# Order of the first loads, folds and weight conversions in a Fourier-mixing and ELU kernel

## The chip, the cores and the metric

The kernel runs on one core of a Trainium2 chip. The core has five engines that work side by side, each through its own list of instructions, in order: TensorE (PE in the profile; PEld is its weight load), VectorE (DVE), ScalarE (ACT), GpSimd (POOL) and SyncE (SP), which here issues most transfers. Transfers run on the core's 16 DMA engines. The metric is the device time of one execution, in microseconds. A kernel's time is the median of several runs.

## The reference

```python
# x: 8 x 3008 x 256 float32; w_in: 256 x 2048, w_out: 2048 x 256
X = np.fft.fft(x, axis=1)
X = np.fft.fft(X, axis=2)
t = X.real.astype(np.float32).reshape(8 * 3008, 256)
h = t @ w_in
g = np.where(h > 0.0, h, np.exp(np.minimum(h, 0.0)) - 1.0)
out = (g @ w_out).astype(np.float32)
```

The real part of a two-dimensional Fourier transform of each batch feeds a two-layer network with an ELU between the layers. The two weights come as 64-bit floating-point numbers, x as 32-bit ones.

## The kernel before, in words

**The transform.** The 3008 rows of a batch are folded. The row s, its mirror image and the two rows half a sequence away are added and subtracted, in both the sequence and the channel direction, so that four short products with cosine and sine matrices are enough. `load_x(b)` brings a batch as four tiles: xl0 and xl3 hold the forward rows and come through SyncE's queue (L197, L198, in `ahead`); xl1 and xl2 hold the backward rows and come by an indirect gather that GpSimd issues (L181, in `back`). `fold_x` makes, for each of the four, an even fold `e0` to `e3` and an odd fold `o0` to `o3` of 128 x 768 elements (all at L504), a copy of one column (`c0` to `c3`), and then the sums E0, E2, EO0, EO1 and O0, O2, EO2, EO3. For batch 0 all folds run on VectorE, in the order in which they are called; for the others they run on GpSimd, in between. `fold_first` adds up one extra channel (`xa`, `xg`, `xd`, `xe`), and a `Dft` multiplies a folded tile with a matrix `MC` (PSUM banks pA to pD, M or H): `x_even` from `xe`, `R_even` from EO0, `I_even` from EO2, `R_odd` from EO1, `I_odd` from EO3. `copy`, `unfold`, `plus` and `minus` bring the result from PSUM into the rings Rr, Ir and Rb.

**The weights.** The transform over the channels is worked into `w_in` instead: `fold_chunk(c)` multiplies the converted chunk c of `w_in` with a constant matrix CC on TensorE, and `put_chunk(c)` copies the result into Wc and Ws. A chunk of 256 columns is loaded raw (512 KB, L238) and converted from 64 to 32 bits in four steps:

- `fields` (VectorE, L256 and L262) cuts out exponent and mantissa.
- `power` (ScalarE) turns the exponent into a power of two; in all chunks but the first two more passes convert the integers.
- `round` joins the two halves of the mantissa: on VectorE in `w_in`'s chunk 0 (L287), on GpSimd in all others.
- `scale` sets the sign in the power (VectorE, L310) and multiplies, on VectorE in chunk 0 (L319), on GpSimd (L419) in the others. In the chunks of `w_in` from 1 on, GpSimd then makes a sum and a difference (`pair`), which `fold_chunk` reads.

**The network.** Work goes in slots. A slot takes 128 x 512 values: `mm_P` (H from Rr and Wc) and `mm_Q` (added to it, from Ir and Ws) on TensorE, `even_part` (E, VectorE, L811), `h_minus` (L821), four passes of ScalarE for the ELU, `g_plus` and `g_minus` (L837), then the products with `w_out` into pA to pD.

**What sets the order.** A hand-written schedule: `at(t, fn)` records each piece with a due time, and at the end all pieces are called in the order of the due times. Almost every instruction is pinned, so the due times settle only the order on each engine; waits are then set for the data. Before the schedule come 46 products of zeros on TensorE and the first loads:

```python
    w1_chunks[0].load()
    nc.sync.dma_start(out=CC, in_=CC_dr.ap())
    L_first, loads = load_x(0)
    for load in loads:
        load()
    load_mats(0, 0, (BE,))
    w1_chunks[1].load()
```

`load_rest` first has ScalarE copy a row of x and write one element of MC10, which holds back that load and the ones behind it until x has come.

Of the kernel before, what the change touches and what calls it, by code (L numbers as in the profile page):

```python
# [72 lines left out]
def _chan_consts():  # L73

    c = np.arange(128)[:, None]

    def block(fn, d):  # L80
        return fn(2.0 * np.pi * ((c * d[None, :]) % 256) / 256)

    even, odd = np.arange(0, 129, 2), np.arange(1, 128, 2)
    return np.concatenate(
        [
            block(np.cos, np.roll(even[:64], -1)),
            -block(np.sin, even[1:64]),
            block(np.cos, even[64:]),
            -block(np.sin, odd),
            block(np.cos, odd),  # L90
            block(np.sin, odd),
            -block(np.cos, odd),
        ],
        axis=1,
    ).astype(np.float32)
# [11 lines left out]
def kernel(  # L107
# [7 lines left out]
    nc = tc.nc  # L115
# [6 lines left out]
    CC_dr = nc.inline_tensor(_chan_consts(), name="chan_mats")  # L122
# [47 lines left out]
    def load_x(b):  # L170

        L = [
            spool.tile([128, 6 * ND], FP, tag=f"xl{j}", bufs=1, name=f"xl{j}")
            for j in range(4)
        ]

        def back(j, few):
            cols = slice(0, 2 * ND) if few else slice(2 * ND, 6 * ND)
            c = 1 if few else 2 if j == 1 and b == NB - 1 else 0
            pin(  # L180
                nc.gpsimd.indirect_dma_start(  # L181
                    out=L[j][:, cols],
                    out_offset=None,
                    in_=xflat,
                    in_offset=bass.IndirectOffsetOnAxis(
                        ap=ix[:, c : c + 1].bitcast(U32), axis=0
                    ),
                    element_offset=(b * SEQ + (HALF if j == 1 else 0)) * ND,
                )
            )  # L190
            if b == NB - 1 and j == 1 and not few:
                nc.gpsimd.dma_start(
                    out=L[1][0:1, 2 * ND : 5 * ND], in_=xrows(b, SEQ - 3, 1, 1, 3)
                )

        def ahead(j, row):
            nc.sync.dma_start(out=L[j][:, 0 : 4 * ND], in_=xrows(b, row, 4, 128, 4))  # L197
            nc.sync.dma_start(  # L198
                out=L[j][:, 4 * ND :], in_=xrows(b, row + 512, 2, 128, 2)
            )  # L200

        loads = [lambda n=n: back(2 - n // 2, n % 2) for n in range(4)]
        return L, loads + [lambda: ahead(3, HALF), lambda: ahead(0, 0)]


    CC = cpool.tile([128, 384], FP, tag="CC")
# [10 lines left out]
    class Chunk:  # L217
# [7 lines left out]
        def load(self):  # L225
            dst = self.dst()
            home = self.home
            if isinstance(home, tuple) and (wide or self.pairs):
                tag, bufs, size = home
                home = spool.tile([128, size], FP, tag=tag, bufs=bufs, name="raw")  # L230
            self.ab = home[:, 0:512]
            if not wide:
                nc.sync.dma_start(out=dst, in_=self.src)
                return
            words = home[:, 0:1024].bitcast(I32)
            self.raw = words.rearrange("p (n w) -> p n w", w=2)
            n = dst.shape[1]
            nc.sync.dma_start(  # L238
                out=words.rearrange("p (a b) -> p a b", a=n), in_=self.src.bitcast(I32)
            )  # L240
# [84 lines left out]
    def w1_dst(c):  # L325
        q, half = divmod(c, 2)
        if q not in w1:
            t = spool.tile([128, 1024], FP, tag="ot", bufs=2, name="w1")
            w1[q] = t.rearrange("p (h n) -> p h n", h=2)
        return w1[q][:, :, half * 256 : (half + 1) * 256]  # L330
# [17 lines left out]
    w1_chunks = [  # L348
        Chunk(
            moe_w_in[:, c * 256 : (c + 1) * 256].rearrange("(h p) n -> p h n", p=128),  # L350
            lambda c=c: w1_dst(c),
            IN_HOMES[c],
            IN_TMP[c],
            c > 0,
            c > 0,
        )
# [21 lines left out]
    def load_mats(ri, kodd, cuts=()):  # L378
        n = (2 * ri + kodd) * BW
        ends = (0, *cuts, BW)  # L380
        for a, z in zip(ends, ends[1:]):
            nc.sync.dma_start(
                out=MC[ri, kodd][:, a:z], in_=MC_dr.ap()[:, n + a : n + z]
            )
# [36 lines left out]
    def act(o, i, func=AF.Copy, **kw):  # L421
        pin(nc.scalar.activation(out=o, in_=i, func=func, **kw))  # L422
# [408 lines left out]
    def exp_neg(ap):  # L831
        act(ap, ap, func=AF.Exp, scale=-1.0)
# [270 lines left out]
    for _ in range(46):  # L1103
        mm(idle, zero, zero[:, 0:1].to_broadcast([128, 512]), True)
    exp_neg(warm)
    w1_chunks[0].load()
    nc.sync.dma_start(out=CC, in_=CC_dr.ap())
    L_first, loads = load_x(0)
    for load in loads:
        load()  # L1110
    load_mats(0, 0, (BE,))
    w1_chunks[1].load()
    nc.sync.dma_start(out=pick, in_=PK_dr.ap())
# [4 lines left out]
    def fold_now(keys):  # L1118
        for key in keys.split():
            ops[key, 0]()  # L1120

    def dft_now(d, par, tag):
        d.mms(par, bank(tag))
# [6 lines left out]
    def at(t, fn):  # L1130
        events.append((t, len(events), fn))
# [10 lines left out]
        for chunk in (w1_chunks[3], w2_chunks[1], w1_chunks[4], w2_chunks[2]):  # L1142
            chunk.load()

    at(-26.0, w1_chunks[0].fields)
    at(-25.9, w1_chunks[0].power)
    at(-25.8, w1_chunks[0].round)
    def begin_x_even():
        state["x_even"] = Dft(0, 0, 0, fold_first(L_first), ring=Rb, first=True)

    at(-25.6, w1_chunks[0].scale)
    at(-25.5, load_rest)
    at(-25.0, lambda: fold_now("e3 c3 e0 c0 e2 c2 E2"))
    at(-24.5, begin_x_even)
    at(-24.4, lambda: fold_now("e1 c1 E0 EO0"))
    at(-20.7, lambda: load_mats(1, 1))
# [6 lines left out]
    at(-13.08, lambda: dft_now(state["x_even"], 1, "pD"))  # L1163
    at(-13.0, lambda: dft_now(R_even, 0, "pA"))
    at(-12.9, lambda: dft_now(R_even, 1, "pB"))
    at(-11.1, lambda: fold_now("o3 o2 O2"))
    at(-11.0, lambda: state["x_even"].unfold())
    at(-10.96, lambda: fold_now("o0 o1 O0 EO2"))
    at(-10.95, R_even.copy)
    at(-10.94, R_even.unfold)  # L1170
    at(-10.9, R_even.plus)
# [7 lines left out]
    at(0.05, lambda: dft_now(I_even, 1, "M"))  # L1179
    at(0.6, lambda: state["x_even"].minus())  # L1180
    at(0.61, lambda: act(Ir[96:128, NE:RUN], Rb[96:128, NE:RUN]))
    at(0.72, w1_chunks[1].scale)
    at(1.3, lambda: fold_now("EO1"))

    T = PERIOD
# [279 lines left out]
```

## Time and profile before

| | |
|---|---|
| time | 1958.78 us, median of 3 runs (1958.31 to 1960.0) |
| span of the profiled execution | 1955.7 us |
| TensorE busy | 1937.6 us, 99% |
| VectorE busy | 1300.7 us, 67% |
| GpSimd busy | 1377.4 us, 70% |
| first product with real data | 13.80 us |
| mean granted TensorE clock | 0.997 of full speed |

The first rows are the whole; the change is in the first 40 us. Until about 37 us the DMA engines move some 400 GB/s without a pause: x, the matrices, and the first half of the weights. The first slots start at 29.7 us, and from about 60 us the profile repeats itself from slot to slot. In a line of the timeline the columns are start in us, duration in us, engine, line, operation, what is written and read, and the number of instructions; in brackets the idle time of the engine just before, and what ended it. When several instructions are in one line, the duration runs from the first start to the last end.

### The profile page before, as it was taken

The numbers are of one execution on the slowest core, as the hardware profiler recorded it, in microseconds if no ns is written. First come the engines' busy times: TensorE is split into PE (matmuls) and PEld (weight loads), VectorE is DVE, ScalarE is ACT, GpSimd is POOL, SyncE is SP. The second block draws the span as 40 slices with busy tenths as digits, with TensorE's granted clock in tenths as the row PEclk, the third lists the DMA queues.
The fourth block names the chain that finished last, engine by engine and source line by source line (L and its number), as shares of the span: only waits on it lengthen the run. The fifth ranks groups of instructions, "written<-read, shape, count | busy, mean of one in ns | idle before, by whom it ended". The sixth has DMA issues, their size and how long they took to land.

```text
span 1955.7 us, 26996 instructions
## 1 busy us (share of the span) xinstructions
PE 1937.6 (99%) x8912; PEld 1655.1 (85%) x8912; DVE 1300.7 (67%) x2396; ACT 864.8 (44%) x1671; POOL 1377.4 (70%) x1816
## 2 busy tenths in 40 slices
PE   7999999999999999999999999999999999999999
PEld 4788788888888888888888888888888888888887
DVE  6976666666666666676666666666666766667666
ACT  3654444444444444444444444444444444344443
POOL 2788668776687766777667876678667777456655
PEclk8999999999999999999999999999999999999999
DMA  8236120111211021010210102002020010100101
GB/s 309 66 25 55 18 65 18 33 28 23 48 20 44 13 41 33 18 44 14 54 23 14 46 13 59 12 19 55 9 54 11 20 22 15 17 12 11 23 10 24
DMA packets 263290, 70.25 MB, mean 36 GB/s; under 512 B 248606, under 2 KB 249522, under 8 KB 263152
## 3 DMA queue, kind: packets, MB, share of 16 engines
q1 hardware_dynamic: 257360, 55.69, 14.7%
q0 software_dynamic: 3616, 12.59, 2.0%
q8 instruction: 70, 1.15, 0.2%
q14 instruction: 68, 0.56, 0.1%
q10 hardware_dynamic: 2176, 0.26, 0.1%
HBM read 43.66 MB, written 24.80 MB: 35 GB/s over the span
## 4 chain that ended last, share of the span: by engine, by line
PE 95%; DVE 2%; POOL 1%; issue 1%; DMA 1%; ACT 0%; SPq 0%; DVEq 0%; POOLq 0%
PE H L410 38%; PE pB L410 16%; PE pC L410 16%; PE pD L410 16%; PE pA L410 8%; POOL WT L419 1%; DMA xl<-in_x_dram 1%; POOL w L419 0%; DVE E L811 0%; POOL G L419 0%; DVE G L837 0%; DVE pow L310 0%; DVE v L416 0%; DVE G L821 0%; ACT G L422 0%
## 5 line engine op out<-in xcount | busy, mean ns | idle before, releaser
L419 POOL TENSOR_TENSOR G<-G 128x256 f32<-128x256 f32 x1440 | 1034.8, 728 | 510.8 <-DVE G L837 341.2
L811 DVE SCALAR_TENSOR_TENSOR E<-Rb,wex,H 128x256 f32<-128x256 f32 x752 | 327.8, 477 | 540.8 <-PE H L410 535.8
L422 ACT ACTIVATE G<-H 128x512 f32<-128x512 f32 x376 | 224.5, 597 | 959.3 <-DVE G L821 959.3
L410 PE MATMUL H<-Ir,Ws 128*128 128x256 f32 x1504 | 388.0, 380 | 2.3 <-DVE E L811 2.3
L410 PE MATMUL H<-Rr,Wc 128*128 128x256 f32 x1504 | 387.1, 380 | 0.0
L410 PE MATMUL pC<-G,WT 128*128 128x256 f32 x1440 | 369.5, 379 | 0.0
L410 PEld LDWEIGHTS H<-Rr,Wc 128*128 128x128 f32 x1504 | 285.1, 190 | 55.7 <-issue 3.3
L410 PEld LDWEIGHTS H<-Ir,Ws 128*128 128x128 f32 x1504 | 278.7, 190 | 51.4 <-DVE E L811 5.5
L410 PEld LDWEIGHTS pC<-G,WT 128*128 128x128 f32 x1440 | 273.6, 190 | 37.2
L821 DVE SCALAR_TENSOR_TENSOR G<-E,H 128x512 f32<-128x512 f32 x376 | 256.8, 683 | 45.6 <-POOL G L419 7.1
L837 DVE SCALAR_TENSOR_TENSOR G<-G,H 128x512 f32<-128x512 f32 x376 | 255.8, 680 | 42.5 <-ACT G L422 42.5
L837 DVE SCALAR_TENSOR_TENSOR G<-M,G 128x512 f32<-128x512 f32 x376 | 256.6, 683 | 0.0
L422 ACT ACTIVATE G<-G 128x512 f32<-128x512 f32 x376 | 233.2, 620 | 0.0
L410 PE MATMUL pD<-G,w 128*128 128x256 f32 x784 | 229.4, 379 | 0.4 <-POOL G L419 0.4
L410 PE MATMUL pA<-G,w 128*128 128x256 f32 x784 | 229.3, 379 | 0.0
L410 PE MATMUL pB<-G,w 128*128 128x256 f32 x784 | 229.3, 379 | 0.0
L422 ACT ACTIVATE M<-G 128x512 f32<-128x512 f32 x376 | 224.3, 596 | 0.0
L422 ACT ACTIVATE M<-M 128x512 f32<-128x512 f32 x376 | 221.0, 588 | 0.1
L410 PE MATMUL pB<-G,WT 128*128 128x256 f32 x720 | 214.8, 380 | 0.3
L410 PE MATMUL pD<-G,WT 128*128 128x256 f32 x720 | 214.1, 379 | 0.0
L410 PEld LDWEIGHTS pD<-G,w 128*128 128x128 f32 x784 | 148.9, 190 | 21.0 <-POOL G L419 0.8
L410 PEld LDWEIGHTS pA<-G,w 128*128 128x128 f32 x784 | 149.0, 190 | 20.2
(148 smaller groups left out, 1420.7 us busy)
## 6 DMA issues: line engine op xcount, KB each, us to landing
out_dram<-ot SPq DMA_DIRECT2D x496, 32.0 KB
xl<-in_x_dram SPq DMA_DIRECT2D x16, 512.0 KB
xl<-in_x_dram SPq DMA_DIRECT2D x16, 256.0 KB
out_dram<-ot SPq DMA_DIRECT2D x256, 2.0 KB
Rb<-r SPq DMA_DIRECT2D x10, 376.0 KB
raw<-in_moe_w_in_dram SPq DMA_DIRECT2D x7, 512.0 KB
MC<-dft_mats SPq DMA_DIRECT2D x3, 943.5 KB
raw<-in_moe_w_out_dram SPq DMA_DIRECT2D x4, 512.0 KB
```

Source lines behind the costliest of these rows:

```text
L410: nc.tensor.matmul(out_, lhsT=lhsT, rhs=rhs, start=start, stop=stop, skip_group_check=True)
L419: pin(nc.gpsimd.tensor_tensor(out=o, in0=a, in1=b, op=op))
L422: pin(nc.scalar.activation(out=o, in_=i, func=func, **kw))
L811: nc.vector.scalar_tensor_tensor(out=S.E[:, c], in0=Rb[:, cols(i)], scalar=wex[:, f : f + 1], in1=S.H[:, c], op0=ALU.mult, op1=ALU.add,)
L821: nc.vector.scalar_tensor_tensor(out=two(S.G[:, 0:512])[:, :, ::-1], in0=two(S.E), scalar=2.0, in1=two(S.H), op0=ALU.mult, op1=ALU.subtract,)
L837: nc.vector.scalar_tensor_tensor(out=o, in0=e, scalar=-1.0, in1=h, op0=ALU.add, op1=ALU.max)
```

## The change

Three things move. On SyncE's queue, xl3 and xl0 of batch 0 come first, ahead of chunk 0 of `w_in` and of CC. On VectorE, the folds of these two tiles, even and odd (e3, o3, e0, o0), come ahead of the conversion of chunk 0, which is then laced with e2 and E2; on ScalarE the column copies c3 and c0 come ahead of chunk 0's power, and the row copy of `load_rest` comes behind c2. And for chunk 1 of `w_in` the `scale` step is due at -10.84 instead of 0.72: its sign (L310) comes in front of the first slot's `even_part` on VectorE instead of behind the second's. No instruction is added or taken away. The order on TensorE and on GpSimd is the same; on SyncE one weight load of the fifth chunk of `w_out`, which waits for a buffer, is now in front of batch 1's xl3 instead of behind it.

The purpose: VectorE is to fold x while it would be waiting for more of it, and GpSimd is to get the sign of chunk 1 in time.

```diff
-    w1_chunks[0].load()
-    nc.sync.dma_start(out=CC, in_=CC_dr.ap())
     L_first, loads = load_x(0)
     for load in loads:
         load()
+    w1_chunks[0].load()
+    nc.sync.dma_start(out=CC, in_=CC_dr.ap())
     load_mats(0, 0, (BE,))
...
-    at(-26.0, w1_chunks[0].fields)
-    at(-25.9, w1_chunks[0].power)
-    at(-25.8, w1_chunks[0].round)
+    at(-26.9, lambda: fold_now("e3 c3 o3 e0 c0 o0"))
+    at(-26.8, w1_chunks[0].fields)
+    at(-26.7, w1_chunks[0].power)
+    at(-26.6, lambda: fold_now("e2 c2"))
+    at(-26.5, w1_chunks[0].round)
+    at(-26.4, lambda: fold_now("E2"))
+    at(-26.3, w1_chunks[0].scale)
...
-    at(-25.6, w1_chunks[0].scale)
     at(-25.5, load_rest)
-    at(-25.0, lambda: fold_now("e3 c3 e0 c0 e2 c2 E2"))
     at(-24.5, begin_x_even)
     at(-24.4, lambda: fold_now("e1 c1 E0 EO0"))
...
-    at(-11.1, lambda: fold_now("o3 o2 O2"))
+    at(-11.1, lambda: fold_now("o2 O2"))
     at(-11.0, lambda: state["x_even"].unfold())
-    at(-10.96, lambda: fold_now("o0 o1 O0 EO2"))
+    at(-10.96, lambda: fold_now("o1 O0 EO2"))
...
-    at(0.72, w1_chunks[1].scale)
+    at(-10.84, w1_chunks[1].scale)
```

## The prediction, made before the changed kernel ran

> **What bounds the kernel now.** I read the page first (how busy the engines are), then the table by stages, then the timeline and the chain of waits of the first 60 us. The page says that TensorE is the bound of the whole:
>
> ```profile
> PE 1937.6 (99%) x8912; PEld 1655.1 (85%) x8912; DVE 1300.7 (67%) x2396; ACT 864.8 (44%) x1671; POOL 1377.4 (70%) x1816
> ```
>
> So only 18 us of the span are TensorE idle, and an edit that leaves the number of matmuls alone can win only there. The table by stages shows where they are (PE is the first busy time after the length of the stretch, PEclk the granted clock, then the DMA share and GB/s):
>
> ```profile
> 20.00:30.00 10.00, 6.88 (x25) 5.12 (x24) 9.60 (x18) 1.66 (x4) 0.00 (x0) 0.84 1.04 405
> 30.00:40.00 10.00, 4.77 (x18) 3.08 (x17) 7.85 (x14) 3.68 (x8) 4.59 (x4) 0.84 0.75 284
> 40.00:50.00 10.00, 9.73 (x40) 6.98 (x40) 6.63 (x13) 6.76 (x15) 4.54 (x5) 0.80 0.39 131
> 50.00:60.00 10.00, 9.71 (x47) 7.37 (x46) 10.00 (x17) 6.23 (x13) 6.31 (x6) 1.00 0.21 53
> 60.00:70.00 10.00, 9.98 (x50) 7.97 (x49) 9.06 (x16) 6.34 (x14) 9.30 (x9) 1.00 0.44 138
> ```
>
> From 20 to 40 us PE misses 8.4 us, from 60 on nothing. Besides, the clock is below 1.00 from 20 to 50. TensorE's own timeline shows the two gaps, and what they cost twice:
>
> ```profile
> 23.46 0.50 PE L410 MATMUL H<-pick,Ws 128*128 128x1 f32 x4
> 27.08 2.86 PE L410 MATMUL pC<-MC,o 128*128 128x189 f32 x6 [3.12 <-issue]
> ...
> 33.66 1.10 PE L410 MATMUL H<-Ir,Ws 128*128 128x256 f32 x4
> 40.27 1.12 PE L410 MATMUL H<-raw,CC 128*64 128x256 f32 x4 [5.50 <-POOL raw L419]
> ```
>
> After 3.12 us idle, six matmuls of I_even take 2.86 us; the same six of R_even take 1.28 in the chain of waits. After 5.50 us idle, the eight of fold_chunk(1) take 1.98 (later chunks: 1.08). The first gap ends when VectorE has made EO2 (26.98). The second is a chain in the timeline of all engines:
>
> ```profile
> 35.02 0.86 DVE L811 SCALAR_TENSOR_TENSOR E<-Rb,wex,H 128x256 f32<-128x256 f32 x2
> 35.80 0.68 DVE L310 SCALAR_TENSOR_TENSOR pow<-raw,pow 128x512 int32<-128x512 int32 x1
> ...
> 36.62 1.32 POOL L419 TENSOR_TENSOR w<-w,pow 128x512 f32<-128x512 f32 x1 [4.25 <-DVE pow L310]
> ```
>
> GpSimd sits idle 4.25 us for a sign that VectorE could have set once ScalarE's power was there (29.91). Then come product and pair (to 40.22), and TensorE. VectorE idles early instead, waiting for x:
>
> ```profile
> 9.05 0.96 DVE L504 TENSOR_TENSOR e<-xl 128x768 f32<-128x768 f32 x1 [1.30 <-DMA xl<-in_x_dram]
> 13.44 1.83 DVE L504 TENSOR_TENSOR e<-xl 128x768 f32<-128x768 f32 x2 [3.44 <-DMA xl<-in_x_dram]
> ```
>
> **What the Trainium skill says.** "TensorE: Matmul & The Clock Gate", Part 1: a free-running window of 3413 ns; after an idle window the array has half the clock, and a busy window gives it back. The trace agrees: read in stretches of 1 us, the clock falls at 26.86, returns at 30.27, falls at 37.10 and returns at 43.92, all multiples of 3.41 apart. It fell after windows with 0.5 and 1.1 us of work and not after one with 2.5; between lies the threshold. "SBUF — State Buffer", Who interferes with whom: a VectorE instruction with two SBUF inputs and a GpSimd instruction that reads SBUF block each other. The trace agrees: EO1 takes 1.48 us beside GpSimd, the same kind 0.96 alone. "DMA: Bandwidth & Descriptors", Queues, rings and completion order: an engine takes packets from its queues in turn, and each ring in order. That fits the landings below, which I use instead of a price.
>
> **Loads.** Landings of before, from what waited for them: the first weights (512 KB) at 4.8; with CC (192) and xl3 (768), 1472 KB in all, at 9.0; with xl0 (768), 2240 KB, at 13.4. GpSimd's gathers share the engines and are not moved. Straight lines between these points give the new order: xl3 (768 KB) 5.9, xl0 (1536) 9.4, first weights (2048) 12.3, CC 13.4. Estimates; plus or minus 1 us. Later loads keep place and bytes, except that xl3 of batch 1 goes behind a weight load that waits until after 35; its first use is after 80. Costs nothing.
>
> **VectorE.** By start-to-start times of before: e3 5.9, o3 6.9, e0 9.4, o0 10.35, done 11.3. These two odd folds (1.8 us) now lie in the old 4.7 us of idle. Then fields 12.35, e2 13.2, round 14.08, E2 14.75, sign 15.65, product 16.37, so w1 chunk 0 is ready at 17.06 (before: 7.75). fold_first to 17.5 (before 16.86), then e1, copy, E0, EO0 as before 3.14 us, to 20.64 (before 20.00). o2, O2 to 22.4, x_even's unfold to 22.9, o1, O0, EO2: R_even's unfold can start at 25.7 (before 26.90). VectorE by itself is 1.2 us ahead, though the even folds are 0.6 late. On ScalarE, copies for e3 and e0 lie in idle time; the row for x1 slips some 1.5 us, which MC10's load hides, as its user comes 12 us later.
>
> **A new wait.** fold_chunk(0) is the first real work on TensorE, and everything is queued behind it in order: x_even, R_even, I_even. The zero matmuls that keep it warm end at 13.87, so it now idles 3.2 us to 17.1. With the old window phase the window 13.21 to 16.62 has 0.66 us of work: half clock until 20.03. Sixteen matmuls need 0.248 us each then (from the eight at 40.27), 0.122 after: done 20.55. pC and pD 3.3 us as before, pA from 23.85, pB's end 27.05 (before 23.62). R_even.plus, which waits for pB, starts at 27.1 instead of 27.61: ahead by 0.5. At full clock it would be 1.2 (VectorE's bound); with weights 1 us late, 0.5 behind. I take 0.5 ahead. The old first gap closes: I_even follows at 27.4, warm.
>
> **The early sign.** 0.68 us on VectorE in front of E, which waited 1.33 us for wex (from ScalarE) anyway: free. The queue behind it is that E, then TensorE's first ring; none moves later. ScalarE's conversion ends at 30.5 (30.99 less 0.5), GpSimd adds 1.30, multiplies 1.30, pairs 2.20: fold_chunk(1) starts at 35.45, not 40.27. TensorE idles from 33.6 for 1.85 us instead of 5.50, so I take it as warm: fold 1.08, Q 1.03, R_odd's pA 1.3, turn 0.34, pB 2.0, to 41.2 (before 47.76); next P to 42.1. Its partners keep up: EO1 by 37.3, ScalarE's four ELU passes 38.1 to 40.2, G at 41.0, w2 chunk 0 on GpSimd at 40.5, all before TensorE asks at 42.1. VectorE: R_odd.unfold 41.0, plus and minus 41.6 to 42.6, sign of chunk 2, E at 43.3 to 44.2; the Q behind it starts at 44.3, before at 50.65. That is 6.35; I take off one GpSimd block of 0.52 (EO1's), so 5.8 us. From 60 on TensorE is full, and VectorE's work is in step with it: the shift stays to the end. 1958.8 - 5.8 = 1953.0.
>
> **Rivals.** (a) Half clock strikes again in the second gap (1.85 us is between the known cases; a half-clock window costs up to 1.7), or the first weights land late (1.0): together some 2.0 less, 1955.0. For: in the old phase that window has 1.65 us of work. Against: that's above the 1.1 which fell. (b) The wait only moves: VectorE, 100% busy from 50 to 60, becomes the bound. In 26 to 52 it is busy 20.2 of 26, so it can give at most 5.8, and if the waits on H and ScalarE stay, about a third: 1956.9. Against: those waits end with TensorE's and ScalarE's own work, which moves too. (c) Slower: the first weights' delay and a worse interlock of VectorE and GpSimd in the 50 us after, ten blocks of 0.5 and 5 more from the late fold_chunk(0): 10 lost against 5.8, 1963. Against: a delay of fold_chunk(0) is paid once, on a chain with over 3 us of old idle behind it. (d) No half clock at all: 1951.7.
>
> **Numbers.** Forecast 0.54, (a) 0.22, (b) 0.13, (c) 0.05, (d) 0.06. Faster by 0.2% means under 1954.9: forecast, (d) and half of (a), 0.71; same 0.24 (the rest of (a), (b)); slower 0.05. Range 1951.5 to 1957.0: it leaves out (c) and the edges. It covers weights late by 1 us, either clock state in both gaps, and up to two thirds lost to VectorE.
>
> **What would show it.** In the trace after: e3 and o3 before 8 us, the first weights' fields near 12.3, fold_chunk(0) near 17 with a clock below 1 behind it, I_even near 27.4 without a gap, fold_chunk(1) near 35.5, the Q of the third step near 44.5, and no idle of 0.5 us beyond that was not there before. Wrong, if fold_chunk(1) starts after 38, if TensorE waits for E or G by more than 1 us between 36 and 60, or if the lead at 60 us is not the lead at the end.

## The result and the profile after

| | before | after |
|---|---|---|
| time, median of 4 runs each | 1959.39 us | 1951.88 us |
| range of the runs | 1958.31 to 1960.21 | 1950.55 to 1953.88 |
| span of the profiled execution | 1955.7 us | 1952.1 us |
| start of the third step's Q in it | 50.65 us | 45.98 us |

The ratio is 0.9963, with an interval of 0.9946 to 0.998: 7.5 us less, and between 4 and 10.6 with the interval. A later comparison (e8 below) gave 6.3 us. The two profiled executions differ by less, 3.6 us: the one of before was quick (1957.48), the one of the changed kernel the slowest of its four (1953.88). The forecast was 1953.0, in a range of 1951.5 to 1957.0.

The page of the changed kernel: TensorE's work is the same to 0.4 us, the span is shorter.

```profile
span 1952.1 us, 26996 instructions
...
PE 1937.2 (99%) x8912; PEld 1654.7 (85%) x8912; DVE 1299.0 (67%) x2396; ACT 864.9 (44%) x1671; POOL 1379.2 (71%) x1816
```

The table by stages of the changed kernel (columns as before: length, busy time of PE, PEld, DVE, ACT and POOL, granted clock, DMA share, GB/s):

```profile
10.00:20.00 10.00, 6.55 (x31) 3.15 (x31) 8.18 (x17) 1.55 (x5) 0.00 (x0) 0.81 1.05 403
20.00:30.00 10.00, 10.00 (x39) 6.84 (x36) 7.82 (x14) 1.83 (x5) 0.00 (x0) 0.85 1.03 404
30.00:40.00 10.00, 8.75 (x42) 6.09 (x41) 8.74 (x20) 5.84 (x14) 5.30 (x6) 1.00 0.70 257
40.00:50.00 10.00, 8.72 (x39) 5.86 (x39) 9.90 (x18) 7.54 (x17) 5.91 (x6) 1.00 0.44 175
50.00:60.00 10.00, 10.00 (x47) 8.45 (x47) 9.06 (x16) 7.92 (x16) 7.25 (x6) 1.00 0.33 91
```

From 20 to 40 us TensorE misses 1.25 us instead of 8.35, but from 10 to 20 it now misses 3.45, where it had missed 1.24, and the half clock now begins there (a granted clock of 0.81, and of 0.85 from 20 to 30). From 40 to 50 VectorE is busy for 9.90 us of 10; whether it is the next bound is tried in e9. TensorE's timeline of the changed kernel:

```profile
17.08 3.68 PE L410 MATMUL H<-w,CC 128*64 128x256 f32 x16 [3.45 <-DVE w L319]
20.69 2.64 PE L410 MATMUL pC<-MC,xe 128*128 128x189 f32 x6
...
28.61 1.52 PE L410 MATMUL pC<-MC,o 128*128 128x189 f32 x6
...
34.13 1.10 PE L410 MATMUL H<-Ir,Ws 128*128 128x256 f32 x4 [0.36 <-DVE Ir L416]
36.12 1.08 PE L410 MATMUL H<-raw,CC 128*64 128x256 f32 x8 [0.89 <-POOL raw L419]
...
43.46 1.97 PE L410 MATMUL pA<-G,w 128*128 128x256 f32 x8 [0.72 <-DVE bs L416]
45.98 1.13 PE L410 MATMUL H<-Ir,Ws 128*128 128x256 f32 x4 [0.56 <-DVE E L811]
```

The two old gaps (3.12 and 5.50) are gone or short. The 0.89 ahead of fold_chunk(1) is the end of GpSimd's chain, which now runs without a hole. At half clock are now fold_chunk(0) (3.68 instead of 1.95) and the first half of x_even (2.64 instead of 1.54).

### The profile page after: what moved, and what is told of

Same layout as the page of the kernel before. It is cut to its first block, busy times and chain, and to the rows that moved or that the text cites. A ratio compares the mean times of both kernels' runs of the same rounds, so it can differ in the third digit from the quotient of the medians.

```text
span 1952.1 us, 26996 instructions
## 1 busy us (share of the span) xinstructions
PE 1937.2 (99%) x8912; PEld 1654.7 (85%) x8912; DVE 1299.0 (67%) x2396; ACT 864.9 (44%) x1671; POOL 1379.2 (71%) x1816
## 4 chain that ended last, share of the span: by engine, by line
PE 93%; DVE 2%; POOL 2%; issue 1%; DMA 1%; ACT 1%; SPq 0%; DVEq 0%; POOLq 0%
PE H L410 37%; PE pC L410 16%; PE pD L410 16%; PE pB L410 16%; PE pA L410 8%; POOL WT L419 1%; POOL w L419 1%; DMA raw<-in_moe_w_in_dram 1%; POOL G L419 1%; DVE E L811 0%; DVE G L837 0%; DMA xl<-in_x_dram,ix 0%; DVE v L416 0%; DVE G L821 0%; DVE pow L310 0%
```

## The experiments

Every time below is a median, with the ratio to the kernel before on the same chip and its interval. "Third Q" is the start of `mm_Q` in the third step in the profiled execution; the time from there to the end of the span varies little: 1905.1 us in the kernel before, 1905.3 in e1 and in e8, 1906.1 in the changed kernel's own profile, and in the others from 1905.1 to 1906.4, but for e3 with 1906.9. So an edit in the front can be judged there, to about 1 us.

### Which part carries the gain: e1 and e2

e1 is the kernel before with the sign of chunk 1 early and nothing else; e2 is the changed kernel with the sign late again.

```diff
-    at(0.72, w1_chunks[1].scale)
+    at(-10.84, w1_chunks[1].scale)     # e1: this line alone; e2: all but this line
```

> Theory (the early sign carries the gain): GpSimd adds at 31.1 as in the kernel before and goes on without a wait to product and pair, 4.1 us as in the changed kernel, so fold_chunk(1) starts near 35.2 instead of 40.27, the clock stays full from there, and the Q of the third step starts near 45 instead of 50.65. The half clock from 26.9 to 30.3 stays. Time 1953.5, within 1 us. Rival (the folds carry it, the sign only fills what they open): under 2 us gained, 1957 or more.

> Theory: loads and folds alone close the first gap, but open one before fold_chunk(0) at 17, and the wait for the sign behind the second step stays with its half clock: fold_chunk(1) near 40, third Q near 50, 1958.5 within 1 us. Rival (the folds carry the gain): 1954 or less.

Measured: e1 1952.57 us, 0.9965 (0.9951 to 0.9979), 6.7 us less. e2 1958.3 us, 0.9996 (0.9987 to 1.0004), no difference that can be told. The rival fell in both: the sign alone has the ratio of the whole change (0.9963), the rest alone has no gain that can be told. GpSimd's timeline in e1:

```profile
32.26 1.29 POOL L419 TENSOR_TENSOR w<-raw,w 128x512 f32<-128x512 f32 x1 [25.46 <-ACT wex L422]
33.63 1.27 POOL L419 TENSOR_TENSOR w<-w,pow 128x512 f32<-128x512 f32 x1
34.98 1.42 POOL L419 TENSOR_TENSOR raw<-w 128x256 f32<-128x256 f32 x2
```

No bracket in the second line: the 4.25 us wait is gone. And TensorE in e1:

```profile
28.25 1.52 PE L410 MATMUL pC<-MC,o 128*128 128x189 f32 x6 [1.43 <-issue]
...
36.45 1.85 PE L410 MATMUL H<-raw,CC 128*64 128x256 f32 x8 [0.88 <-POOL raw L419]
...
46.72 1.13 PE L410 MATMUL H<-Ir,Ws 128*128 128x256 f32 x4 [0.28 <-DVE E L811]
```

fold_chunk(1) starts at 36.45, not at 35.2, because xl0 came later in this execution than in the profile of before (VectorE starts e0 at 14.61, there at 13.44). Two things that the expectation said of the clock failed in this execution, the slowest of e1's five. The first half clock came from 19.6 to 23.0 and not behind the first gap, so I_even ran at full clock. And half clock followed the new, short gap too, from 36.6 to 40.0: the eight products took 1.85 us instead of 1.08. So here the early sign took away the wait, not the half clock behind it, and the third Q is still 3.9 us earlier than before. In e2 the old wait stands, whatever the folds did ahead of it:

```profile
41.14 1.98 PE L410 MATMUL H<-raw,CC 128*64 128x256 f32 x8 [5.50 <-POOL raw L419]
```

### How much of the sign's gain is the clock: e5

The kernel before, with the late sign, and 17 products of zeros on TensorE in the second gap.

```diff
+    def keep_warm(tag, n):
+        ps = bank(tag)
+        for _ in range(n):
+            mm(ps, zero, zero[:, 0:1].to_broadcast([128, 512]), True)
+    at(2.295, lambda: keep_warm("pA", 17))
```

> The kernel before, sign still late, with 17 products of zeros (some 4.6 us) on TensorE in the gap ahead of fold_chunk(1), so that its clock stays full there. They write a bank that nobody reads. Theory (of the 6.7 us that the early sign brings, the wait itself is 4.2 to 5 and the half clock behind it up to 1.7): fold_chunk(1) still near 40.3, but eight products in 1.08 and R_odd's pA near 42.4 instead of 44.0; 1957.6. Rival (the clock is hidden by VectorE's work in the third step): 1959. Second rival (the clock is most of it): 1955 or less.

Measured: 1957.04 us, 0.9992 (0.9984 to 1.0): 1.75 us less, with an interval from 0 to 3.1. Its timeline shows the eight products at full clock in spite of the late start, but not what is behind them:

```profile
36.40 3.86 PE L410 MATMUL pA<-zero 128*128 128x512 bf16 x16
42.05 1.08 PE L410 MATMUL H<-raw,CC 128*64 128x256 f32 x8 [1.79 <-POOL raw L419]
43.07 1.66 PE L410 MATMUL H<-Ir,Ws 128*128 128x256 f32 x4
44.52 2.63 PE L410 MATMUL pA<-MC,e 128*128 128x188 f32 x6
```

Half clock set in at 43.5 and held to 46.9: Q took 1.66 us instead of 1.13 and R_odd's pA 2.63 instead of 1.43. In this execution, one of the two slowest of 13 (1959.75 us, mean clock 0.997), the zeros only put the half clock off. The six executions with 0.999 average 1956.7, which is 2.1 under the median of before. So the zeros seem to have spared some executions the half clock and others not, and the gain of 1.75 us does not measure it cleanly. It has the size that the theory gave, about a quarter of the sign's 6.7 us, but its interval just touches no gain at all, and in e1 half clock followed the new gap too. How the 6.7 us divide between the wait and the clock stays open.

### What the folds and the new load order lose on TensorE: e3, e6, e7, e11

e3 is the changed kernel with 57 zero products at the start instead of 46.

```diff
-    for _ in range(46):
+    for _ in range(57):
```

> The changed kernel with 57 zero matmuls instead of 46, so that they end near 16.7, just ahead of the first weights at 17.08. Theory (the half clock before fold_chunk(0) costs, and its phase makes the spread between executions): clock 1.00 throughout, fold_chunk(0) in 1.95 us instead of 3.7, pB ends near 25.6 instead of 28.3, R_even.plus starts at 26.5 by VectorE; 1950.3, and the executions lie within 1 us of each other. Rival (VectorE and ScalarE set the pace, the clock is hidden): 1951.9, spread as before.

Measured: 1952.79 us, 0.9964 (0.9951 to 0.9978). The expectation failed, but so did the experiment: the zeros ended at 15.9, the weights were ready only at 18.1 in the profiled execution, and the clock fell all the same, at 19.3 to 22.7. Three executions with a mean clock of 0.999 averaged 1953.6, the two with 1.000 averaged 1951.5. That is a hint that the half clock costs here too, not more.

e6 puts fold_chunk(0) on TensorE behind R_even, so that x_even and R_even don't queue behind it. e7 has, besides, chunk 1's conversion in VectorE's hole. e11 is e6 with ScalarE's copies of the result further back.

```diff
-    at(-13.2, lambda: fold_chunk(0))
-    at(-13.1, lambda: put_chunk(0))
+    at(-12.85, lambda: fold_chunk(0))
+    at(-10.93, lambda: put_chunk(0))        # e6, e7; e11: at -10.865
...
-    at(-10.88, w1_chunks[1].fields)         # e7 alone
+    at(-11.05, w1_chunks[1].fields)         # power -11.04, round -11.03, scale -10.97
...
-    at(0.05, lambda: dft_now(I_even, 1, "M"))   # e11 alone
+    at(-10.4, lambda: dft_now(I_even, 1, "M"))  # turn_last_row(0) behind it
```

> The changed kernel with fold_chunk(0) on TensorE behind R_even's products instead of ahead of x_even's, and the copy of its result behind R_even.copy on ScalarE. Theory (the folds' 1.2 us on VectorE are eaten because x_even and R_even queue behind fold_chunk(0), which comes late and at half clock): pB ends 2 to 3.7 us earlier, near 24.7, R_even.plus starts near 26.8 instead of 28.4, as soon as VectorE is there; 1950.5, that is 1.2 to 1.6 under the changed kernel. Rival (the arrival of x sets the pace, not TensorE's queue): no difference, 1951.9.

> As the one with fold_chunk(0) late, and all of chunk 1's conversion in the hole that VectorE has ahead of x_even.unfold. Theory (GpSimd's chain for chunk 1 is the wait that is left, 0.9 us ahead of fold_chunk(1)): no wait there; up to 0.9 under the one with fold_chunk(0) late, 1949.6. Rival (GpSimd's three operations now lie beside VectorE's folds and block them, 0.5 us each): 1951 or more.

> fold_chunk(0) behind R_even on TensorE again, but with ScalarE's copies of its result behind chunk 1's three passes and I_even's second half ahead of the first P, so that nothing on ScalarE waits for it. Theory (the folds' lead on VectorE is lost to TensorE's queue, and in the first try was lost again to ScalarE's queue): R_even.plus near 26.7, GpSimd's first sum for chunk 1 near 30.0 instead of 31.0, fold_chunk(1) near 34.4 instead of 35.2; 1951.5. Rival (VectorE's E and I_even's unfold set the third step whatever comes before): 1952.3 or more.

Measured: e6 1953.35 us, 0.9972 (0.9962 to 0.9982); e7 1953.9 us, 0.9975 (0.9965 to 0.9986); e11 1954.15 us, 0.9973 (0.9962 to 0.9984). None gained on the changed kernel (1951.88, and 1952.5 in e8); all three expectations failed in the time. The mechanism showed: R_even.plus starts at 26.60 in e6 and at 26.07 in e11, where it had been 28.45 and 27.55 in the two profiles of the changed kernel. The lines of e6 and e11:

```profile
26.60 0.55 DVE L416 TENSOR_TENSOR Rr<-bs,pB 128x377 f32<-128x377 f32 x1 [0.31 <-PE pB L410]
26.07 0.55 DVE L416 TENSOR_TENSOR Rr<-bs,pB 128x377 f32<-128x377 f32 x1
```

In both the lead was lost again later. ScalarE in e6:

```profile
24.69 0.33 ACT L422 ACTIVATE anti<-pA 128x189 f32<-128x189 f32 x1 [3.91 <-PE pA L410]
28.48 0.38 ACT L422 ACTIVATE Ws<-H 128x256 f32<-128x256 f32 x1 [3.46 <-PE H L410]
...
29.16 0.51 ACT L422 ACTIVATE Ir<-Rb 32x377 f32<-32x377 f32 x1
29.70 0.72 ACT L422 ACTIVATE pow<-pow,ebias 128x512 int32<-128x512 int32 x1
```

The copy waits 3.46 us for TensorE, and chunk 1's power, for which VectorE had everything ready at 28.3, queues behind it. In e11 that is mended, and GpSimd's first sum starts at 29.55 (expected 30.0), but then VectorE's first E waits for the first P. That P needs the copies, which end at 30.00, and it stands on TensorE behind I_even's second half (28.70 to 30.77), where this edit put it; it starts at 30.97:

```profile
28.41 0.69 DVE L310 SCALAR_TENSOR_TENSOR pow<-raw,pow 128x512 int32<-128x512 int32 x1
32.19 0.87 DVE L811 SCALAR_TENSOR_TENSOR E<-Rb,wex,H 128x256 f32<-128x256 f32 x2 [3.09 <-PE H L410]
```

In e7 the wait ahead of fold_chunk(1) is gone as expected (35.19, directly behind a Q), and the third Q is at 46.02 all the same: TensorE then waits for E, for EO1 and for the bank pA, which R_odd's unfold frees, all from VectorE. The rival of e7 showed as well. Beside GpSimd's three operations the two odd sums on VectorE, from 25.17 on, took 3.87 us instead of the 1.95 of e6, and R_even.plus came only at 29.67.

### Is the new load order needed: e4 and e10

e4 has the old loads, weights first, the early sign, and of the folds only o3 in the early hole. e10 is e4 with the third step's E ahead, as in e9.

```diff
-    at(-25.0, lambda: fold_now("e3 c3 e0 c0 e2 c2 E2"))
+    at(-25.0, lambda: fold_now("e3 c3 o3 e0 c0 e2 c2 E2"))
-    at(-11.1, lambda: fold_now("o3 o2 O2"))
+    at(-11.1, lambda: fold_now("o2 O2"))
-    at(0.72, w1_chunks[1].scale)
+    at(-10.84, w1_chunks[1].scale)
```

> The kernel before with the old loads and weights first, and only o3 moved, into VectorE's idle time ahead of e0, and the early sign. Theory (one odd fold of 0.9 us fits without delaying fold_chunk(0), which stays at 13.8): EO2 ends near 26.1, I_even at 26.1 behind an idle time of 2.2 us, fold_chunk(1) near 34.4, third Q near 44.3; 1952.5, a little under the sign alone, and 1951 if the clock stays up. Rival (the new order of the loads is needed): same time as the sign alone, 1953.5 or more.

> The old order of loads, o3 in VectorE's early idle time, the early sign, and E of the third step ahead. Theory (order of the loads is worth nothing beside the sign): the same as the changed kernel with the third step's E ahead, 1951.4. Rival (the new load order matters): 1952.5 or more.

Measured: e4 1952.41 us, 0.9966 (0.9954 to 0.9978); e10 1952.46 us, 0.9961 (0.9947 to 0.9975). Neither can be told from the changed kernel, nor e4 from the sign alone, nor e10 from e9 (0.996 below), its counterpart with the new order, though e10's time is nearer its rival's figure than its theory's. No run shows that the new order is needed. Whether o3 itself brings anything stays open: e4's profile, of its fastest execution, in which xl0 came early (e0 at 13.18), has the earliest third Q of all, 44.06; its median doesn't follow.

### The next bound: e9 and e12; the same again: e8

From 36 to 46 us the changed kernel's VectorE is busy for 9.90 us of 10. TensorE's last wait in that stretch is for E of the third step, which stands behind R_odd.plus and minus. e9 puts it ahead of them; e12 adds that to e11; e8 is the changed kernel itself, on the chip of e5 to e7. The diff is e9's.

```diff
+        if slot == 2:
+            begin = ((-0.7, mm_P), (-0.575, even_part)) + begin[2:]
...
-        (T + 4.2, R_odd.plus),
-        (T + 4.21, R_odd.minus),
+        (T + 4.24, R_odd.plus),
+        (T + 4.25, R_odd.minus),
```

> The changed kernel, with the sign of chunk 2 and then E of the third step on VectorE ahead of R_odd.plus and minus (1.0 us) instead of behind them. Theory (after the change the next bound is VectorE between 36 and 46, and TensorE's last wait there, 0.57, is for this E): the Q of the third step starts 1.0 us earlier by this trace, 44.1 against 45.1 at the same arrival of x, and the lead stays; 1951.5, about 1.0 under the changed kernel. Rival (the next product waits for the bank that plus and minus free, or fold_chunk(2) for GpSimd, and the lead is gone by 50 us): 1952.3.

> Both: fold_chunk(0) late with its copies behind, and the third step's E ahead. Theory (the two gains lie on different stretches and add up): 1950.6. Rival (one chain, the larger gain only): 1951.5.

> The changed kernel on the same chip as these three. Both theories: 1951.9, within 1 us; executions with clock 1.000 lie 1 to 2 us under those with 0.998.

Measured: e9 1952.04 us, 0.996 (0.9946 to 0.9974); e12 1954.01 us, 0.9971 (0.996 to 0.9983); e8 1952.5 us, 0.9969 (0.9957 to 0.9982). e9 lies between its theory and its rival, and e12 missed both of its figures: if anything, it is slower than the changed kernel. In e9's TensorE timeline the Q comes without a wait, 0.8 us earlier than in e8 (first line), and most of that is gone at the next Q, which is at 51.38 instead of 51.63:

```profile
45.08 1.13 PE L410 MATMUL H<-Ir,Ws 128*128 128x256 f32 x4 [0.57 <-DVE E L811]
...
44.25 1.03 PE L410 MATMUL H<-Ir,Ws 128*128 128x256 f32 x4
45.11 1.89 PE L410 MATMUL pB<-G,w 128*128 128x256 f32 x8
47.13 1.08 PE L410 MATMUL H<-raw,CC 128*64 128x256 f32 x8
...
51.38 1.13 PE L410 MATMUL H<-Ir,Ws 128*128 128x256 f32 x4 [0.37 <-DVE E L811]
```

What may remain is a quarter to half a microsecond (the two spans are 1949.9 and 1950.4), which five executions do not show. So no version here is shown to beat the changed kernel.

## Why the prediction was right, and where its account was not

**Bound and carrier.** Right. The gain came from TensorE's idle time and half clock in the first 50 us, and the lead at the third Q is the lead at the end, to about 1 us. In the changed kernel's own profile 1.1 us of the 4.67 went back later, in part in two new waits for GpSimd (0.56 ahead of fold_chunk(3), 0.8 in the middle of the run where it had been 0.4). One of the signs of success failed: TensorE has two idle times of over 0.5 us that were not there before, the 0.72 and the 0.56 (before 0.29) for VectorE in its timeline above.

**Loads.** Forecast first uses 5.9, 9.4, 12.3; measured 5.18, 9.13, 12.60. The straight lines between old landings served.

**VectorE.** Forecast w1 chunk 0 at 17.06 and fold_chunk(0) at 17.1; measured 17.08. Its timeline in the changed kernel shows the odd folds in what had been idle time:

```profile
9.13 0.96 DVE L504 TENSOR_TENSOR e<-xl 128x768 f32<-128x768 f32 x1 [2.12 <-DMA xl<-in_x_dram]
10.00 0.95 DVE L504 TENSOR_TENSOR o<-xl 128x768 f32<-128x768 f32 x1
12.60 0.43 DVE L256 TENSOR_SCALAR pow<-raw 128x512 int32<-128x512 int32 x1 [1.64 <-DMA raw<-in_moe_w_in_dram]
```

**The new wait was undersized.** The sum for pB's end was 0.14 us short (23.85 and the 3.34 of before make 27.19, not 27.05). The half clock was to end at 20.03 and R_even.plus to be 0.5 us ahead of before. In the changed kernel's profile the half clock lasted two windows, to 22.9, and plus, at 28.45, was 0.8 behind; in e8, with one window, it started at 27.55, 0.1 ahead:

```profile
27.11 0.61 DVE L416 TENSOR_TENSOR bs<-pA,anti 128x189 f32<-128x189 f32 x2
28.45 0.55 DVE L416 TENSOR_TENSOR Rr<-bs,pB 128x377 f32<-128x377 f32 x1 [0.73 <-PE pB L410]
```

In e8 plus waited just as long for pB, 0.74. That VectorE's lead is eaten in TensorE's queue is shown by e6 and e11, where plus comes earlier; the 1.2 us themselves were not measured alone. That loads and folds together are worth next to nothing is shown by e2 (0.8 us less, within an interval that holds zero).

**The early sign.** Right in kind and nearly in size: fold_chunk(1) forecast at 35.45, measured 36.12 and 35.20, and warm, as I took it. The reason given for that does not hold, and that it came true was in part luck. Against rival (a), half clock in this gap, the prediction said that a window with 1.65 us of work is above the 1.1 after which the clock fell. In e1 it fell after a window with 1.46, in e5 after one with 1.62. In the changed kernel's profile it stayed up, and the window, 33.18 to 36.59, held 2.16 us. The sum gave the early sign 5.3 of 5.8 us (the other 0.5 was to come from the folds); alone it brought 6.7 (4 to 9.6 with the interval).

**The block by GpSimd** was taken off at 0.52. EO1 was not held up (0.95). A block came elsewhere and larger: L262 of chunk 2 took 1.50 instead of 0.42, beside an operation of GpSimd from 39.98 to 41.32:

```profile
40.10 1.50 DVE L262 TENSOR_SCALAR w<-raw 128x512 int32<-128x512 int32 x1
```

Forecast third Q 44.8 with the block, measured 45.98 and 45.08.

**Profiles against medians.** By single profiles the shift at the third Q was 4.7 and 5.6, a little under the forecast of 5.8; the medians moved by 7.5 and 6.3, a little over, and the intervals hold 5.8. The profile of before is of an execution (1957.48) quicker than any other on record of that kernel, whose medians are 1958.8 to 1959.4. I read the waits from that one and subtracted them from a median. Whether this made the sum too small is not shown: the same wait of 5.50 us stands in e2's profile, of a slow execution (1960.11). What makes up the rest of the medians' shift stays open. Rivals (b) and (c) fell: VectorE did fill up from 40 to 50, but the gain stayed.

## What to carry to other kernels

A short instruction that another engine waits for, queued behind work that nobody is waiting for, is worth moving by itself: here the late place of an instruction of 0.68 us on VectorE held up GpSimd for 4.25 us and TensorE for 5.5, with half clock behind it. Filling an engine's idle time pays only if nothing that the first consumer needs is put later: the folds were to bring VectorE 1.2 us forward, and TensorE, which now waited over 3 us for the weights and had half clock behind that, took it back. Before a forecast is drawn from one profile, compare its time with the median of the kernel.

## What the runs showed that I had not expected

- A window need not be idle for the clock to fall, and half clock outlasts a well-filled one. The clock changes at distances that are multiples of 3.41 us, so the stretches are cut there. It fell after stretches in which TensorE was busy 1.46 us (e1, 33.21 to 36.62) and 1.62 us (e5, 40.11 to 43.52), with no single idle time over 1.8 us; it stayed up after 2.16 (changed kernel) and 2.54 (before, first line below). In the changed kernel half clock held from 16.12 to 22.94, two stretches, though TensorE was busy 2.45 us of the first (the other lines); in the kernel before it ended after a stretch with 3.19.

```profile
13.21:16.62 3.41, 2.54 (x20) 1.16 (x17) 2.90 (x5) 1.61 (x7) 0.00 (x0) 1.00 1.04 395
...
16.12:19.53 3.41, 2.45 (x12) 1.46 (x14) 3.27 (x9) 0.00 (x0) 0.00 (x0) 0.50 1.09 398
19.53:22.94 3.41, 3.41 (x12) 2.19 (x9) 2.78 (x3) 0.66 (x2) 0.00 (x0) 0.50 1.02 424
```

- The mean clock of an execution counts the stretches at half clock. By an estimate from 3.41 us and the span, each takes 0.09% from the mean: the profile of before has three and 0.997, the changed kernel's two and 0.998, e8's one and 0.999. The ten executions of the changed kernel, sorted by it: 1950.55 at 1.000, six that average 1952.0 at 0.999, three that average 1953.5 at 0.998. A stretch seems to cost about 1.5 us. That is a hint only: in e1 and in e4 the execution with 1.000 is not the quickest.
- The same loads in the same order land at different times: the first weights' use started at 12.60, 12.83, 13.63 and 13.90 in the changed kernel, e8, e3 and e2, and e0 with the old order at 13.44, 14.61, 13.18 and 14.26 in the kernel before, e1, e4 and e10. That spread of up to 1.4 us is as much as most edits here could bring, and limits what five executions can tell. It is not simply handed on: of the first three, the changed kernel's profile has the earliest weights and the latest third Q (45.98, against 45.08 and 45.86), with half clock for two stretches and not one.
